# Attention over packs and a two-matrix FFN on one Trainium2 core: from batch 3 on the first softmax is turned by VectorE and small DMAs, side products stand in pairs, and x @ w_in runs two units ahead

## The chip, the core and the metric

The kernel runs on one core of a Trainium2 chip. Its engines are PE (matmul), ACT (activations, copies, casts), DVE (elementwise work, reductions and transposes of 32x32 blocks), POOL (little used here) and SP, whose queue issues nearly all DMAs. The metric is the device time of one execution in microseconds.

## The reference

Eight batches with eight heads of 64, 576 tokens each. 32 packs per head attend to the tokens; the tokens then attend to the 32 results; what comes out goes through an FFN with 2048 hidden columns.

```python
def sm_attn(qq, kk, vv):                       # softmax(qq kk^T / 8) vv, float32
    s = scale * np.matmul(qq, kk.transpose(0, 1, 3, 2))
    ...
p_packed = sm_attn(p, k, v)                    # 32 rows per head
out = sm_attn(q, p_packed, p_packed)           # 576 rows per head
x = out.transpose(0, 2, 1, 3).reshape(4608, 512)
h = x @ w_in                                   # 512 x 2048
return (h * sigmoid(h)) @ w_out                # 2048 x 512
```

## The kernel before

**Units.** The bulk of the work is 128 units, one for a batch and a block of 128 hidden columns, 16 a batch. x itself is never formed. As a token's row of x is its second softmax (32 shares per head) times the packs, `packs_in` multiplies the packs of a batch with w_in once, a quarter (512 columns) at a time, into `pw`. `h_unit(u)` then multiplies `pw` with the shares `a2` (12 matmuls of 288 columns, the line with `a_hi`, `a_lo`, `pw_hi`, `pw_lo`, L408); ACT takes silu out of PSUM three times (`g`, `g_hi`, and `rest` for the 64 tokens that don't fill a block), and DVE makes `g_lo`, the part that `g_hi` lost in rounding. `out_unit(u)` multiplies `g` with w_out (12 matmuls of 512 columns, L422) and sums in PSUM over the 16 units of a batch. Every second batch has four more units for the rest rows (`(b, f, "rest")`).

**Side work.** During the units of batch b the attention of batch b + 1 is made by the generator `side`, piece by piece: scores of packs and keys in two halves (`heads`, L212), maximum on DVE, exponentials on ACT (L251), ten transposes of the exponentials on PE (L274, L279) with copies back to SBUF, the packed product with the values (L289), one more transpose (L308), the second scores in two halves (L212), their softmax (DVE turns blocks of 32, so that a token's 32 shares lie in a row), and four quarters of `packs_in` (L212). Each piece has one two-bank PSUM buffer from a ring of one (`ps_side`); x @ w_in has another (`ps_hid`), and the output sums have the remaining four banks (`ps_acc`).

**Order.** In the first 32 units (batches 0 and 1, `BLOCKS`, while the weights come in and are put together by `Weights`), a scheduler orders all engines by its own estimate of times. Afterwards PE follows the source (`manual_schedule` for PE alone), and the other engines' order is still the scheduler's. `h_unit(u + 1)` stands ahead of `out_unit(u)`: the distance is one unit.

**Start.** Before the first unit, `keep_warm` puts blocks of matmuls on the identity between the pieces of batch 0's attention (`WARM`: 16, 7, 3, 4 and 3 of them, then 10). Each takes a new buffer `ps_hid`. Of a float32 matmul there are two records in the trace. Loads, scalings (L168, L169) and joins (L174 to L178) of the weights are pinned behind named steps (`PINS`).

Of the kernel before, what the change touches and what calls it, by code (L numbers as in the profile page):

```python
# [9 lines left out]
F32 = mybir.dt.float32  # L10
F32R = mybir.dt.float32r
# [3 lines left out]
AF = mybir.ActivationFunctionType  # L15
ALU = mybir.AluOpType
AX = mybir.AxisListType
PSUM = bass.MemoryType.PSUM

P = 128  # L20
B, H, S, D = 8, 8, 576, 64
NP = 32
NI = H // 2
HS = S // 2
NB = HS // 32
# [3 lines left out]
NJ = 4  # L29
JW = DFF // NJ  # L30
FJ = JW // P
# [5 lines left out]
EARLY = 2  # L37
BLOCKS = [(0, 0), (0, 1), (1, 0), (1, 1), (1, 2), (0, 2), (0, 3), (1, 3)]
# [13 lines left out]
A1 = range(0, 6)  # L52
A2 = range(15, 32)
KV2 = 12
SCALE = 1.0 / math.sqrt(D)
EPS = 1e-9

# [4 lines left out]
def packed_attention_ffn(ctx: ExitStack, tc: tile.TileContext, pkT, qT, vA, vB, w_in, w_out, out):  # L62
# [10 lines left out]
    nc = tc.nc  # L73
    ent = ctx.enter_context
    const = ent(tc.tile_pool(name="const", bufs=1))
    kvq = ent(tc.tile_pool(name="kvq", bufs=2))
    pw = ent(tc.tile_pool(name="pw", bufs=2))
    a2p = ent(tc.tile_pool(name="a2p", bufs=4))
    tmp = ent(tc.tile_pool(name="tmp", bufs=2))
    small = ent(tc.tile_pool(name="small", bufs=2))  # L80
    gp = ent(tc.tile_pool(name="gp", bufs=2))
# [14 lines left out]
    made = {}  # L96

    def keep_warm(times):

        with after("pe"):  # L100
            for _ in range(times):
                ps = ps_h.tile([P, 2, 512], F32, name="ps_hid")
                made["pe"] = nc.tensor.matmul(ps[:, 0, :P], ident, ident, start=True, stop=True)  # L103

    def after(name):
        return tc.issue_after(made[name].ins) if name in made else nullcontext()

    def load_pk(b):
        t = kvq.tile([P, 5 * DM], F32, name="kvq_t")
        n = P + NI * HS  # L110
        for c in (slice(0, n), slice(n, n + NI * HS)) if b == 0 else (slice(0, P + NI * S),):
            nc.sync.dma_start(t[:, c], pkT[b, :, c])
        return t[:, :P], t[:, P : P + NI * S].rearrange("p (hf i s) -> p hf i s", hf=2, i=NI)

    def load_q(b):
        t = kvq.tile([P, 5 * DM], F32, name="kvq_t")
        n = NI * HS
        for c in (slice(0, n), slice(n, 2 * n)) if b == 0 else (slice(0, 2 * n),):
            made["q_load", b] = nc.sync.dma_start(t[:, c], qT[b, :, c])
            if b == 0 and c.start == 0:  # L120
                weights.fetch(1)
        return t[:, : NI * S].rearrange("p (hf i s) -> p hf i s", hf=2, i=NI)

    def load_v(b):
        t = kvq.tile([P, 5 * DM], F32, name="kvq_t")
        nc.sync.dma_start(t[:, : 4 * DM], vA[b])
        nc.sync.dma_start(t[: S - 4 * P, 4 * DM :], vB[b])
        return t.rearrange("p (c e) -> p c e", c=5)

    class Weights:  # L130
# [7 lines left out]
        def __init__(self, stage):  # L138
            self.stage, self.raw, self.n, self.fetched = stage, {}, 0, 0

            rings = [["stage", "stage", NJ - 2, NJ - 1], ["stage", "stage", NJ - 1], ["stage", "stage"]]
            self.place, self.after = [], []
            for n in range(len(self.chunks)):
                first = (0, 8, 12)[(n >= 8) + (n >= 12)]
                ring = rings[(n >= 8) + (n >= 12)]
                place = ring[(n - first) % len(ring)]
                before = [m for m in range(n) if self.place[m] == place]
                self.after.append((before[-2:-1] if place == "stage" else before[-1:]) or [-3])
                self.place.append(place)
# [51 lines left out]
    def side_banks(b):  # L201

        if b:
            return ps_s.tile([P, 2, 512], F32, name="ps_side")
        return ps_acc.tile([P, 2, 512], F32, name="ps_acc")

    def heads(bank, lhs, rhs, n):

        for par in range(2):
            r = slice(D * par, D * par + D)  # L210
            for i in range(NI):
                made["pe"] = nc.tensor.matmul(  # L212
                    bank(par)[NP * i : NP * i + NP, :n], lhs(r, i), rhs(r, i), start=True, stop=True
                )

    def scratch(n):
        return tmp.tile([P, 2 * 5 * P], F32, name="tm")[:, : 2 * n]

    def attention(b):
# [134 lines left out]
            made["kv", b + 1] = k_next, load_v(b + 1)  # L354
        yield

    def load_kv(b):
        made["kv", b] = load_pk(b), load_v(b)

    def packs_in(b, j):  # L360
        ps = side_banks(1)
        heads(lambda par: ps[:, par], made["packs", b], lambda r, i: win[r, j, i, :].bitcast(F32), JW)
        pool = pw if b < EARLY or j in (0, NJ - 1) else pw_b
        hi = pool.tile([P, 2, JW], F32R, name="pw_hi")
        lo = pool.tile([P, 2, JW], F32R, name="pw_lo")
        nc.scalar.copy(hi, ps)  # L366
        nc.vector.tensor_tensor(lo, ps, hi.bitcast(F32), ALU.subtract)  # L367
        made["pw", b, j] = hi, lo

    def side(b):  # L370

        yield from attention(b)
        for j in range(NJ):
            packs_in(b, j)
            yield from [None] * 3

# [8 lines left out]
    behind = {}  # L387
# [2 lines left out]

    def h_unit(u):
        b, f, *more = units[u]
        g_hi = gp.tile([P, 512], F32R, name="g_hi")
        g_lo = gp.tile([P, 512], F32R, name="g_lo")
        hidden[u] = g_hi, g_lo
        if more:
            g = rest[:, f : f + FJ].rearrange("p f e h s -> p (f e h s)")
            nc.scalar.copy(g_hi, g)
            nc.vector.tensor_tensor(g_lo, g, g_hi.bitcast(F32), ALU.subtract)
            return  # L400
        p_hi, p_lo = made["pw", b, f // FJ]
        cols = slice(f % FJ * P, f % FJ * P + P)
        ps = ps_h.tile([P, 2, 512], F32, name="ps_hid")
        for hf in range(2):
            a_hi, a_lo = made["a2", b, hf]
            todo = [(p, a, par) for par in range(2) for p, a in ((p_hi, a_hi), (p_hi, a_lo), (p_lo, a_hi))]
            for n, (p, a, par) in enumerate(todo):
                nc.tensor.matmul(ps[:, hf, :HS], p[:, par, cols], a[:, par], start=(n == 0), stop=(n == len(todo) - 1))  # L408
        g = gp.tile([P, 512], F32, name="g", bufs=1)
        main = ps[:, :, :MAIN]  # L410
        silu = nc.scalar.activation(g.rearrange("p (h s) -> p h s", h=2), main, AF.Silu)  # L411
        nc.scalar.activation(g_hi.rearrange("p (h s) -> p h s", h=2), main, AF.Silu)  # L412
        nc.scalar.activation(rest[:, f, b % 2], ps[:, :, MAIN:HS], AF.Silu)  # L413
        lo = nc.vector.tensor_tensor(g_lo, g, g_hi.bitcast(F32), ALU.subtract)  # L414
        behind[u] = silu, lo
# [48 lines left out]
    def load_parts(b):  # L464
        for h in range(2):
            o = osb.tile([P, 2, DM], F32, name="o")
            nc.sync.dma_start(o, parts[b, h])
            outs["o", b, h] = o
# [31 lines left out]
    steps = iter(STEPS)  # L500
    due = next(steps)
    ahead = attention(1)
    ordered = ExitStack()
    for u in range(len(units)):
        b, f, *more = units[u]
        if u < n_early:
            for _ in range(3 if u in A1 else 1 if u in A2 else 0):
                next(ahead, None)
            while u == due:
                silu, lo = behind[u]  # L510
                with tc.issue_after(silu.ins), tc.issue_after(lo.ins):
                    weights.step()
                due = next(steps, None)
            if u % FJ == FJ - 2 and u < n_early - FJ:
                packs_in(*BLOCKS[u // FJ + 1])
            if u == KV2:
                load_kv(2)
                ahead = attention(2)
            if u == n_early - 2:
                packs_in(2, 0)  # L520
            if u % FJ == FJ - 2 and BLOCKS[u // FJ] in ((0, NJ - 1), (1, NJ - 1)):
                load_parts(b)
        else:
            if u == n_early:
                ordered.enter_context(tc.manual_schedule(engines={mybir.EngineType.PE}))
                scope.close()
                pw_b = ent(tc.tile_pool(name="pw_b", bufs=2))
            if u < n_early + FJ - 1:
                packs_in(2, u - n_early + 1)
            if not more and f == 0:  # L530
                for _ in ahead:
                    pass
                ahead = side(b + 1) if b + 1 < B else iter(())
            if not more:
                next(ahead, None)
        if u + 1 < len(units):
            h_unit(u + 1)
        if u >= n_early and not more:
            next(ahead, None)
        out_unit(u)  # L540
    ordered.close()


def _laid_out(q, k, v, p, moe_w_in, moe_w_out):
# [37 lines left out]
```

## Time and profile before

| | us |
|---|---|
| median of 3 runs | 766.7 (765.19 to 766.7) |
| profiled execution | 764.94, its span 763.1 |
| PE busy | 740.8 (97%) |
| weight load (PEld) busy | 580.8 (76%) |
| ACT busy | 345.6 (45%) |
| DVE busy | 328.3 (43%) |
| mean granted clock | 0.981 |

The shares are of the span. A matmul's record includes its way through the array and overlaps the next one's, so the distance between starts says more about PE than the busy share. Where the prediction shows rows of the chain of waits, the columns are the start, the length, and the engine with the tile and line of what was on the chain; rows of the timeline have the start, the length, engine and line, operation, output and inputs, shapes and count.

### The profile page before, as it was taken

Reading aid. Unit: us, or ns where it says so; the run is one execution under the profiler, and the core shown is the slowest. Engines: PE = TensorE matmul, PEld = TensorE weight load, DVE = VectorE, ACT = ScalarE, POOL = GpSimd, SP = SyncE. Lnnn points to the kernel's source line nnn. Section 1 sums busy time; section 2 is a strip of 40 time slices with the busy share of each in tenths; the row PEclk is TensorE's granted clock in tenths of the full one; section 3 lists DMA queues with packets and bytes.
Section 4 is the critical chain, followed back from the end, with each engine's and each line's share of the span. In section 5 each row is a group of like instructions: output and inputs, shape, how many; then the busy total and the mean of one; then the engine's idle time right before and its main releaser. Section 6 shows DMA issues by size and latency. Waiting matters only on the chain.

```text
span 763.1 us, 11971 instructions
## 1 busy us (share of the span) xinstructions
PE 740.8 (97%) x5102; PEld 580.8 (76%) x5102; DVE 328.3 (43%) x482; ACT 345.6 (45%) x606; POOL 17.2 (2%) x14
## 2 busy tenths in 40 slices
PE   8689999999999999999999999999999999999997
PEld 5357767787776887888778787788778887788886
DVE  1697765555754335233713336232723226221112
ACT  2448655754643545362633535353633536242232
POOL 0020000001000000000000000000000000000000
PEclk9958999999999999999999999999999999999999
DMA  6855251334131211031101211031101200010001
GB/s 247 345 179 207 82 165 56 117 111 178 63 110 56 78 66 63 1 118 67 64 0 56 77 67 63 1 118 66 63 1 56 76 2 1 1 56 1 1 1 69
DMA packets 13012, 60.00 MB, mean 79 GB/s; under 512 B 1440, under 2 KB 1440, under 8 KB 8096
## 3 DMA queue, kind: packets, MB, share of 16 engines
q1 hardware_dynamic: 12864, 59.12, 21.5%
q8 instruction: 40, 0.66, 0.4%
q10 hardware_dynamic: 96, 0.13, 0.1%
q14 instruction: 12, 0.10, 0.0%
HBM read 47.71 MB, written 11.53 MB: 78 GB/s over the span
## 4 chain that ended last, share of the span: by engine, by line
PE 86%; ACT 6%; DVE 5%; issue 2%; POOL 0%; ACTq 0%; POOLq 0%
PE ps_acc L422 49%; PE ps_hid L408 26%; PE ps_side L212 6%; PE ps_hid L103 3%; PE ps_side L289 2%; ACT tm L251 1%; ACT L411 1%; ACT L251 1%; DVE mx L241 1%; ACT g L411 1%; ACT g_hi L412 1%; DVE wo_lo L187 1%; DVE g_lo L414 0%; DVE win L177 0%; PE ps_acc L212 0%
## 5 line engine op out<-in xcount | busy, mean ns | idle before, releaser
L422 PE MATMUL ps_acc<-wo_hi,g_hi 128*128 128x512 f32 x576 | 233.6, 406 | 3.2 <-ACT g_hi L412 2.7
L422 PE MATMUL ps_acc<-wo_lo,g_hi 128*128 128x512 f32 x576 | 227.6, 395 | 0.4 <-DVE wo_lo L187 0.4
L422 PE MATMUL ps_acc<-wo_hi,g_lo 128*128 128x512 f32 x576 | 223.5, 396 | 0.0
L411 ACT ACTIVATE g<-ps_hid 128x512 f32<-128x512 f32 x128 | 76.7, 599 | 251.7 <-PE ps_hid L408 248.0
L414 DVE TENSOR_TENSOR g_lo<-g,g_hi 128x512 fp32r<-128x512 f32 x128 | 89.2, 696 | 233.9 <-ACT g_hi L412 233.9
L408 PE MATMUL ps_hid<-a_hi,pw_hi 128*128 128x288 f32 x512 | 156.2, 305 | 2.4 <-ACT rest L413 2.3
L408 PE MATMUL ps_hid<-a_lo,pw_hi 128*128 128x288 f32 x512 | 152.3, 297 | 2.6 <-DVE a_lo L347 2.6
L408 PE MATMUL ps_hid<-a_hi,pw_lo 128*128 128x288 f32 x512 | 151.5, 296 | 0.0
L422 PEld LDWEIGHTS ps_acc<-wo_hi,g_hi 128*128 128x128 f32 x576 | 108.5, 188 | 48.9 <-issue 19.3
L422 PEld LDWEIGHTS ps_acc<-wo_hi,g_lo 128*128 128x128 f32 x576 | 108.4, 188 | 27.3 <-issue 3.0
L422 PEld LDWEIGHTS ps_acc<-wo_lo,g_hi 128*128 128x128 f32 x576 | 108.8, 189 | 20.6 <-DVE wo_lo L187 0.9
L408 PEld LDWEIGHTS ps_hid<-a_hi,pw_hi 128*128 128x128 f32 x512 | 97.1, 190 | 24.6 <-issue 10.1
L408 PEld LDWEIGHTS ps_hid<-a_lo,pw_hi 128*128 128x128 f32 x512 | 97.2, 190 | 7.0 <-DVE a_lo L347 3.0
L408 PEld LDWEIGHTS ps_hid<-a_hi,pw_lo 128*128 128x128 f32 x512 | 97.1, 190 | 0.0
L412 ACT ACTIVATE g_hi<-ps_hid 128x512 fp32r<-128x512 f32 x128 | 75.9, 593 | 0.0
L367 DVE TENSOR_TENSOR pw_lo<-ps_side,pw_hi 128x1024 fp32r<-128x1024 f32 x32 | 39.0, 1220 | 38.6 <-ACT pw_hi L366 38.6
L366 ACT CAST pw_hi<-ps_side 128x1024 fp32r<-128x1024 f32 x32 | 32.4, 1011 | 32.4 <-PE ps_side L212 17.2
L212 PE MATMUL ps_side<-win,ppT 64*32 64x512 f32 x512 | 39.8, 612 | 4.6 <-DVE win L178 4.6
L103 PE MATMUL ps_hid<-ident 128*128 128x128 f32 x86 | 29.4, 437 | 3.4 <-POOL ident masks.py:199 1.4
L103 PEld LDWEIGHTS ps_hid<-ident 128*128 128x128 f32 x86 | 18.4, 266 | 17.6 <-PE ps_hid L103 11.3
L413 ACT ACTIVATE rest<-ps_hid 128x64 f32<-128x64 f32 x128 | 29.5, 230 | 0.0
L411 ACT ACT_TABLE_LOAD x21 | 26.9, 1283 | 5.4 <-PE ps_hid L408 5.2
(93 smaller groups left out, 463.7 us busy)
## 6 DMA issues: line engine op xcount, KB each, us to landing
kvq_t<-in_pkT SPq DMA_DIRECT2D x7, 1216.0 KB, 5.8
w_raw<-in_w_in SPq DMA_DIRECT2D x8, 1024.0 KB, 5.4
kvq_t<-in_vA SPq DMA_DIRECT2D x8, 1024.0 KB, 5.2
out<-o SPq DMA_DIRECT2D x16, 512.0 KB, 2.8
kvq_t<-in_qT SPq DMA_DIRECT2D x7, 1152.0 KB, 5.3
win<-in_w_out SPq DMA_DIRECT2D x5, 1024.0 KB, 4.8
w_raw<-in_w_out SPq DMA_DIRECT2D x3, 1024.0 KB, 4.8
parts<-o SPq DMA_DIRECT2D x4, 512.0 KB, 5.7
```

The lines of the kernel that those rows point to most:

```text
L103: made["pe"] = nc.tensor.matmul(ps[:, 0, :P], ident, ident, start=True, stop=True)
L212: made["pe"] = nc.tensor.matmul(bank(par)[NP * i : NP * i + NP, :n], lhs(r, i), rhs(r, i), start=True, stop=True)
L251: made["exp"] = nc.scalar.activation(e, s, AF.Exp, bias=nm[:, c], scale=SCALE, accum_out=den[:, c])
L289: made["pe"] = nc.tensor.matmul(psp[NP * i : NP * i + NP, par * D : par * D + D], e1T[:n, par, c, NP * i : NP * i + NP], v[:n, c, h * D : ...
L366: nc.scalar.copy(hi, ps)
L367: nc.vector.tensor_tensor(lo, ps, hi.bitcast(F32), ALU.subtract)
L408: nc.tensor.matmul(ps[:, hf, :HS], p[:, par, cols], a[:, par], start=(n == 0), stop=(n == len(todo) - 1))
L411: silu = nc.scalar.activation(g.rearrange("p (h s) -> p h s", h=2), main, AF.Silu)
L412: nc.scalar.activation(g_hi.rearrange("p (h s) -> p h s", h=2), main, AF.Silu)
L413: nc.scalar.activation(rest[:, f, b % 2], ps[:, :, MAIN:HS], AF.Silu)
L414: lo = nc.vector.tensor_tensor(g_lo, g, g_hi.bitcast(F32), ALU.subtract)
L422: nc.tensor.matmul(bank, g[:, rows], w[:, f], start=(first and n == 0), stop=(last and n == 2))
```

## The change

1. `keep_warm` takes one buffer for a whole block of warm-up matmuls.
2. From batch 3 on, the class `Attention` takes the place of the generator; its steps stand at fixed units of the batch before (`STEPS_AT`: unit number to step). The exponentials of the first softmax are turned by DVE in blocks of 32x32 (`turned1`), and sixteen DMAs from SBUF to SBUF, 32 partitions each, put the blocks where PE's transposes had put them. The ten transposes on PE and the two copies behind them are gone.
3. Both halves of the first scores stand together, likewise those of the second scores, and the quarters 0 and 1, and 2 and 3, of `packs_in` (units `PACKS_NEXT` and `PACKS_OWN`). For this `two_banks` gives the two PSUM buffers `ps_hid` and `ps_side` in turn to side pieces and x @ w_in alike. At these units the unit's `h_unit` is left to the next one, which then makes two.
4. x @ w_in stands two units ahead (`hidden_up_to(u + 2)`), with a third buffer for `g_hi`, `g_lo` and for `pw` (`gp_b`, `pw_b`).
5. From the end of the first 32 units, PE, DVE, ACT and SP all follow the source.

```diff
     def keep_warm(times):
+        ps = ps_h.tile([P, 2, 512], F32, name="ps_hid")
         with after("pe"):
             for _ in range(times):
-                ps = ps_h.tile([P, 2, 512], F32, name="ps_hid")
                 made["pe"] = nc.tensor.matmul(ps[:, 0, :P], ident, ident, start=True, stop=True)
...
+STEPS_AT = {1: "scores1", 2: "exps1", 3: "turned1", 7: "packed", 9: "scores2", 10: "exps2", 11: "shares2", 12: "split2"}
+PACKS_NEXT, PACKS_OWN = 13, 4
...
+    turns = [ps_h, ps_s]
+    def two_banks():
+        turns.reverse()
+        return turns[0].tile([P, 2, 512], F32, name="ps_hid" if turns[0] is ps_h else "ps_side")
...
+        def turned1(self):
+            turn = scratch(S)
+            blocks = turn.rearrange("p (t r x) -> p t r x", r=2, x=NP)
+            for par in range(2):
+                nc.vector.transpose(blocks[:, :, par], self.e1[:, par].rearrange("p (t x) -> p t x", x=NP))
+            self.e1T = scratch(5 * P).rearrange("p (c i rx) -> p c i rx", c=5, i=NI)
+            for i in range(NI):
+                for at in range(P // NP):
+                    some = turn[NP * i : NP * i + NP].rearrange("p (t rx) -> p t rx", rx=2 * NP)[:, at :: P // NP]
+                    nc.sync.dma_start(self.e1T[NP * at : NP * at + NP, : some.shape[1], i], some)
...
+    def packs_in(b, *quarters):
+        banks = [side_banks(1) if (b, j) < (EARLY, 1) else two_banks() for j in quarters]
+        for j, ps in zip(quarters, banks):
+            heads(lambda par: ps[:, par], made["packs", b], lambda r, i: win[r, j, i, :].bitcast(F32), JW)
+        for j, ps in zip(quarters, banks):
+            ...   # hi on ACT, lo on DVE, as before
...
+    ent(tc.manual_schedule(engines={E.PE, E.DVE, E.Activation, E.SP}))
...
+        all_banks = step in ("scores1", "scores2") or f == PACKS_OWN or f == PACKS_NEXT and b + 1 < B
+        if not all_banks:
+            hidden_up_to(u + 2)
+        if f == 0 and b + 1 < B:
+            coming = Attention(b + 1)
+        if f == PACKS_OWN:
+            packs_in(b, *((3,) if b == 2 else (2, 3)))
+        if f == PACKS_NEXT and b + 1 < B:
+            packs_in(b + 1, 0, 1)
+        if step:
+            getattr(coming, step)()
         out_unit(u)
+        if step == "packed":
+            coming.packs()
```

**The start on PE**, with buffer numbers: the last warm-up matmuls of the first block, then the first scores, before.

```order
L103 MATMUL ps_hid_137<-ident_88 128x128
L103 MATMUL ps_hid_139<-ident_88 128x128
L103 MATMUL ps_hid_141<-ident_88 128x128
L212 MATMUL ps_acc_143<-kvq_t_103 32x288 x4
L212 MATMUL ps_acc_144<-kvq_t_103 32x288 x4
```

The same place in the changed kernel, from its first matmul to the second block of warm-ups.

```order
L107 MATMUL ps_hid_111<-ident_88 128x128 x16
L223 MATMUL ps_acc_128<-kvq_t_103 32x288 x4
L223 MATMUL ps_acc_129<-kvq_t_103 32x288 x4
L223 MATMUL ps_acc_128<-kvq_t_103 32x288 x4
L223 MATMUL ps_acc_129<-kvq_t_103 32x288 x4
L107 MATMUL ps_hid_146<-ident_88 128x128 x7
```

The matmuls are the same; sixteen buffers have become one.

**Ahead of the first products, on DVE**: `a_lo` is the second half of batch 0's shares, `mx` the maximum of batch 1's first scores, `wo_lo` a part of w_out. Before:

```order
L342 STREAM_TRANSPOSE tm<-tm 128x576
L233 COPY tm<-ps_side 128x2x288
L187 TENSOR_TENSOR wo_lo<-win,wo_hi 128x1024
L241 TENSOR_REDUCE mx<-tm 128x2
L347 TENSOR_TENSOR a_lo<-tm,a_hi 128x576
```

and in the changed kernel:

```order
L181 TENSOR_SCALAR win<-win 128x1024
L244 COPY tm<-ps_side 128x2x288
L358 TENSOR_TENSOR a_lo<-tm,a_hi 128x576
L252 TENSOR_REDUCE mx<-tm 128x2
L191 TENSOR_TENSOR wo_lo<-win,wo_hi 128x1024
```

The scheduler has put `a_lo` ahead of the other two. On ACT, at the same place, before (L251 are batch 1's exponentials, `g` and `g_hi` the first unit's silu):

```order
L251 ACTIVATE tm,den<-tm,nm 128x576 x2
L411 ACT_TABLE_LOAD
L411 ACTIVATE g<-ps_hid 128x512
L412 ACTIVATE g_hi<-ps_hid 128x512
L413 ACTIVATE rest<-ps_hid 128x64
```

and now:

```order
L538 ACT_TABLE_LOAD
L538 ACTIVATE g<-ps_hid 128x512
L539 ACTIVATE g_hi<-ps_hid 128x512
L540 ACTIVATE rest<-ps_hid 128x64
L172 ACTIVATE w_raw<-w_raw 128x1024
L173 ACTIVATE w_raw<-w_raw 128x1024
L172 ACTIVATE w_raw<-w_raw 128x1024
L173 ACTIVATE w_raw<-w_raw 128x1024
L190 CAST wo_hi<-win 128x1024
L262 ACT_TABLE_LOAD
L262 ACTIVATE tm,den<-tm,nm 128x576 x2
L538 ACT_TABLE_LOAD
```

The exponentials have moved from ahead of the first silu to between the first and the second.

**A steady batch.** On PE, one quarter of the packs' product before, between output matmuls (`ps_acc`) and x @ w_in (`ps_hid`):

```order
L422 MATMUL ps_acc<-wo_lo,g_hi 128x512
L422 MATMUL ps_acc<-wo_hi,g_lo 128x512
L212 MATMUL ps_side<-win,ppT 32x512 x8
L408 MATMUL ps_hid<-a_hi,pw_hi 128x288
L408 MATMUL ps_hid<-a_lo,pw_hi 128x288
```

and two quarters in the changed kernel:

```order
L549 MATMUL ps_acc<-wo_hi,g_lo 128x512
L223 MATMUL ps_side<-win,ppT 32x512 x8
L223 MATMUL ps_hid<-win,ppT 32x512 x8
L549 MATMUL ps_acc<-wo_hi,g_hi 128x512
L549 MATMUL ps_acc<-wo_lo,g_hi 128x512
```

The two stand together, in both buffers, between two units' output matmuls. On DVE, from the first scores to the packed product, before:

```order
L241 TENSOR_REDUCE mx<-tm 128x2
L242 TENSOR_SCALAR nm<-mx 128x2
L253 TENSOR_SCALAR rd<-den 128x2
L254 RECIPROCAL rd<-rd 128x2
L414 TENSOR_TENSOR g_lo<-g,g_hi 128x512
L280 COPY tm<-ps_side 64x2x128
L414 TENSOR_TENSOR g_lo<-g,g_hi 128x512 x2
L297 TENSOR_TENSOR pp<-ps_side,rd 128x128
```

and now:

```order
L385 TENSOR_REDUCE mx<-tm 128x2
L386 TENSOR_SCALAR nm<-mx 128x2
L541 TENSOR_TENSOR g_lo<-g,g_hi 128x512 x2
L397 TENSOR_SCALAR rd<-den 128x2
L398 RECIPROCAL rd<-rd 128x2
L541 TENSOR_TENSOR g_lo<-g,g_hi 128x512
L406 STREAM_TRANSPOSE tm<-tm 128x18x32 x2
L500 TENSOR_TENSOR pw_lo<-ps_hid,pw_hi 128x1024
L500 TENSOR_TENSOR pw_lo<-ps_side,pw_hi 128x1024
```

The two turns (L406) are new; the rounding rests of two quarters of `pw` now stand right behind them. On SP the sixteen DMAs (L411) stand between a batch's query load and the next batch's load of packs and keys.

More of the change, by code (lines that the diff above doesn't have):

```diff
@@ L357, in load_kv @@
     def load_kv(b):
         made["kv", b] = load_pk(b), load_v(b)
[L360 to L375, printed above, removed]
+    def packs_in(b, *quarters):
[3 more added lines that the diff above has]
+        for j, ps in zip(quarters, banks):
+            n = NJ * (b - EARLY) + j
+            pool = pw_b if n > 0 and n % 3 == 1 else pw
+            hi = pool.tile([P, 2, JW], F32R, name="pw_hi")
+            lo = pool.tile([P, 2, JW], F32R, name="pw_lo")
+            nc.scalar.copy(hi, ps)
+            nc.vector.tensor_tensor(lo, ps, hi.bitcast(F32), ALU.subtract)
+            made["pw", b, j] = hi, lo
@@ L392, in h_unit @@
         b, f, *more = units[u]
-        g_hi = gp.tile([P, 512], F32R, name="g_hi")
-        g_lo = gp.tile([P, 512], F32R, name="g_lo")
+        pool = gp_b if u > n_early and (u - n_early) % 3 == 1 else gp
+        g_hi = pool.tile([P, 512], F32R, name="g_hi")
+        g_lo = pool.tile([P, 512], F32R, name="g_lo")
         hidden[u] = g_hi, g_lo
@@ L402, in h_unit @@
         cols = slice(f % FJ * P, f % FJ * P + P)
-        ps = ps_h.tile([P, 2, 512], F32, name="ps_hid")
+        ps = ps_h.tile([P, 2, 512], F32, name="ps_hid") if u < n_early else two_banks()
         for hf in range(2):
@@ L502, in packed_attention_ffn @@
     ahead = attention(1)
-    ordered = ExitStack()
-    for u in range(len(units)):
-        b, f, *more = units[u]
[L506 to L523, printed above, removed]
-            if u == n_early:
[L525 to L539, printed above, removed]
@@ new lines, in packed_attention_ffn @@
+    for u in range(n_early):
+        b, f = units[u]
+        for _ in range(3 if u in A1 else 1 if u in A2 else 0):
+            next(ahead, None)
+        while u == due:
+            silu, lo = behind[u]
+            with tc.issue_after(silu.ins), tc.issue_after(lo.ins):
+                weights.step()
+            due = next(steps, None)
+        if u % FJ == FJ - 2 and u < n_early - FJ:
+            packs_in(*BLOCKS[u // FJ + 1])
+        if u == KV2:
+            load_kv(2)
+            ahead = attention(2)
+        if u == n_early - 2:
+            packs_in(2, 0)
+        if u % FJ == FJ - 2 and BLOCKS[u // FJ] in ((0, NJ - 1), (1, NJ - 1)):
+            load_parts(b)
+        h_unit(u + 1)
+        out_unit(u)
@@ new lines, in packed_attention_ffn, with hidden_up_to @@
+    for _ in ahead:
+        pass
+    E = mybir.EngineType
+    ent(tc.manual_schedule(engines={E.PE, E.DVE, E.Activation, E.SP}))
+    scope.close()
+    pw_b = ent(tc.tile_pool(name="pw_b", bufs=1))
+    gp_b = ent(tc.tile_pool(name="gp_b", bufs=1))
+    done = n_early
+    def hidden_up_to(u):
+        nonlocal done
+        while done < min(u, len(units) - 1):
+            done += 1
+            h_unit(done)
+    coming = None
+    for u in range(n_early, len(units)):
+        b, f, *more = units[u]
+        if more:
+            if u == n_early:
+                packs_in(2, 1, 2)
+            else:
+                hidden_up_to(u + 2)
+            out_unit(u)
+            continue
+        step = STEPS_AT.get(f) if b + 1 < B else None
+        all_banks = step in ("scores1", "scores2") or f == PACKS_OWN or f == PACKS_NEXT and b + 1 < B
+        if not all_banks:
+            hidden_up_to(u + 2)
+        if f == 0 and b + 1 < B:
[6 more added lines that the diff above has]
+            getattr(coming, step)()
@@ L540, in packed_attention_ffn @@
         out_unit(u)
-    ordered.close()
+        if step == "packed":
+            coming.packs()
 def _laid_out(q, k, v, p, moe_w_in, moe_w_out):
```

95 lines of the change are left out of this document (added).

## Prediction

> **What bounds the kernel now.** I read the page first, then the windows by stage, then the chain of waits in one steady batch and in the start, then PE's timeline around single pieces.
>
> ```profile
> span 763.1 us, 11971 instructions
> PEclk9958999999999999999999999999999999999999
> PE 86%; ACT 6%; DVE 5%; issue 2%; POOL 0%; ACTq 0%; POOLq 0%
> ...
> 0.00:76.00 76.00, 63.04 (x463) 41.72 (x463) 46.55 (x69) 36.15 (x50) 7.73 (x9) 0.82 0.66 244
> 435.60:517.67 82.07, 81.80 (x604) 65.33 (x604) 31.53 (x49) 37.48 (x70) 0.00 (x0) 1.00 0.16 58
> ```
>
> PE carries 86% of the chain. In a steady batch it has work for 81.80 of 82.07 us, while DVE (31.53) and ACT (37.48) are under half busy: only taking work or gaps out of PE's own stream shortens that part. The first 76 us are different: 13 us without PE work, and a mean clock of 0.82.
>
> **Steady part: the price of a side piece.** The chain of waits in that batch, then PE's timeline around the transposes of the first softmax:
>
> ```profile
> 455.95 2.79 PE ps_acc L422 x12
> 458.74 1.70 PE ps_hid L408 x12
> 460.44 0.65 PE ps_side L212 x16
> 461.09 2.97 PE ps_acc L422 x12
> 464.06 1.02 PE ps_side L212 x16
> 465.08 1.80 PE ps_hid L408 x12
> ...
> 499.65 1.59 PE ps_hid L408 x12
> ...
> 517.45 0.22 PE ps_side L279 x2
> ...
> 514.29 1.03 PE L274 MATMUL ps_side<-ident,tm 128*128 128x128 f32 x8
> 515.59 0.40 PE L408 MATMUL ps_hid<-a_hi,pw_hi 128*128 128x288 f32 x1 [0.27 <-ACT rest L413]
> ```
>
> Undisturbed, a unit is 1.59 (twelve x @ w_in matmuls) and 2.79 (twelve output matmuls), 4.38 us; sixteen are 70.1, so this batch spends 12.0 on side work. A quarter of the packs' product costs 1.02, and the L408 group behind it takes 1.80 instead of 1.59: 1.23. A score piece costs 0.65 + 2.97 - 2.79 = 0.83. The transposes cost more than their matmuls: from 514.29 to 517.45 pass 3.16 us with one L408 group in them, so 1.57 with ACT's 0.27; L279 adds 0.22, and some 0.1 to the group behind it, half of what a longer piece adds: 1.9 a batch.
>
> Two pieces that stand together slow the group behind them once instead of twice (0.2 saved) and let the array run empty once. For the second there are rows at half clock, two score pieces together and one alone, which lasts to the next start:
>
> ```profile
> 14.96 2.10 PE ps_acc L212 x32
> ...
> 43.27 1.21 PE L212 MATMUL ps_side<-kvq_t 64*32 64x288 f32 x16
> 44.41 1.65 PE L103 MATMUL ps_hid<-ident 128*128 128x128 f32 x4
> ```
>
> 2 x 1.14 - 2.10 = 0.18. A merged pair saves 0.2 + 0.17 = 0.37; bounds 0.18 (one effect alone) and 0.5.
>
> **Terms of the steady part**, batches 3 to 7:
> - Transposes off PE: 5 x 1.9 = 9.4 us; bounds 5 x 1.0 (their matmuls alone) and 5 x 2.0.
> - Merged pairs: two of scores and two of quarters a batch, 20 x 0.37 = 7.4; bounds 3.6 and 10. Quarters 1 to 3 of batch 2 stay single in PE's order.
> - x @ w_in two units ahead: the two L408 groups a batch that take 1.70 because ACT has not emptied the bank lose 0.11 each: 1.
> - DVE gains two transposes of 128x576 and loses one copy; ACT loses a copy of 128x1024 and, as the exponentials stand in pairs, two table loads. Both engines are under half busy, so this costs nothing while their order holds (a rival below).
> Together 17.8 us.
>
> **The sixteen small DMAs** of a batch, 32 partitions with runs of 256 bytes, have no like in the trace. Nearest are the stores out of SBUF from the same queue:
>
> ```profile
> L459 SPq DMA_DIRECT2D out<-o x16: 372/394/401, 214.1 to 749.1; - x16
> L439 SPq DMA_DIRECT2D out<-o x14: 332/418/2013, 247.5 to 760.2; - x14
> ...
> DMA to landing us min/median/max: 1.6/2.7/5.0
> ...
> L342 DVE STREAM_TRANSPOSE tm<-tm 128x576 f32<-128x576 f32 x2 | 1.5, 774 | 0.0
> ```
>
> L459 has 256 runs, against 160 or 128 here, so I take its 0.39 an issue: 6.3, and 2.7 to land, 9.0 us; bounds 16 x 0.33 + 1.6 = 6.9 and 16 x 2.01 + 5.0 = 37. What covers it: the exponentials stand in the unit after the scores, behind two silus and a table load, and DVE's two turns (1.55) behind them and the g_lo of the third unit; an estimate from the order puts their end 6.7 us into that unit. The packed product stands behind the seventh unit's L408 group, 4 x 4.38 + 2.1 (two quarters) + 1.59 = 21.2 after the same point. That leaves 14.5 us for 9.0: cost 0. Behind the turns on DVE stand the two pw_lo of the quarters, whose banks PE wants one output group later; behind the DMAs on SP only the next batch's packs and keys, wanted ten units later.
>
> **The start.** The chain of waits of the first 80 us, a window, the first loads and ACT:
>
> ```profile
> 1.36 0.81 PE ps_hid L103 x2
> ...
> 21.14 0.44 PE ps_acc L264 x4
> ...
> 29.02 0.73 PE ps_acc L212 x16
> ...
> 51.22 1.38 DVE wo_lo L187
> 52.60 1.26 DVE mx L241
> 53.87 0.66 DVE a_lo L347
> ...
> 54.70 1.63 ACT tm L251 x4
> ...
> 56.35 1.28 ACT L411
> ...
> 58.78 2.07 PE ps_acc L422 x4
> 60.85 2.34 PE ps_hid L408 x12
> ...
> 65.27 0.93 PE ps_acc L422 x4
> ...
> 30.00:54.50 24.50, 16.77 (x96) 8.43 (x95) 24.33 (x35) 10.57 (x12) 5.13 (x2) 0.60 0.52 181
> ...
> 0.73 0.87 SPq L112 DMA_DIRECT2D kvq_t<-in_pkT  x2
> 2.12 0.59 SPq L126 DMA_DIRECT2D kvq_t<-in_vA  x1
> ...
> kvq_t<-in_vA SPq DMA_DIRECT2D x1, 1024.0 KB, 9.7
> kvq_t<-in_pkT SPq DMA_DIRECT2D x1, 640.0 KB, 3.9
> kvq_t<-in_pkT SPq DMA_DIRECT2D x1, 576.0 KB, 4.8
> ...
> 9.80 1.10 ACT L169 ACTIVATE w_raw<-w_raw 128x1024 f32<-128x1024 f32 x1
> ```
>
> The change's words do not tell of this term. Each of the first sixteen warm-up matmuls takes a new buffer from a ring of one and so waits for the one before: 13.6 us to 14.96, while the keys, issued by 1.6 and 4.8 in flight, had landed by 6.4. The change gives all sixteen one buffer. Back to back a record takes 0.11 (0.44 for four), or 0.22 at half clock, so 32 end between 5 and 8.4.
>
> From there, step by step. The first exponentials stand on ACT behind the first weight scaling, which ends at 10.9 and does not move; the first ends near 11.8, and the transposes run then instead of at 21.14 (seven more warm-ups held them, 4.1 us from 17.06). Copies and values (landed by 12.4) allow the packed product near 14.6, and two shorter warm-up blocks the second scores near 18 instead of 29.02: 11 us earlier. From there to a_lo's end at 54.53 DVE is the bound, busy 24.33 of 24.50 us, and its new order puts wo_lo (1.38) and the maximum (1.26) behind a_lo: a_lo ends near 41. On ACT the first silu no longer stands behind batch 1's exponentials, so products start near 44 instead of 58.78. Then ACT gives part back: between the first and the second silu it now has four scalings (4.4), a cast of about 1, two table loads (2.6) and the exponentials (1.6), so the second unit's products come near 54.3 instead of 65.27. Of that shift of 11 I take off 1 for PE waits behind ACT: **10 us**; bounds 0 (loads set the pace) and 13. Further on the early order is nearly the old one, so the shift stays.
>
> A rule of the Trainium skill speaks against the shorter warm-up: "TensorE: Matmul & The Clock Gate", section "What's actually happening", has PE fall to half clock after an idle window of about 3.4 us, and back after as long a busy one. The trace agrees that the clock falls (PEclk shows 5 in its third slice). By that rule the longer idle stretches of the new start keep the clock down longer: the third rival.
>
> **Sum.** 17.8 + 10 = 27.8 off the profiled execution's 764.94 (its span 763.1 and 1.8 around it): 737.1. The median of the runs, 766.7, lies 1.8 above that execution, so **739 us**.
>
> **Rivals.**
> - *The small DMAs land late* (slower than before). PE then waits at the packed product of five batches. The whole gain is gone when they take 14.5 + 27.8 / 5 = 20 us, which is 1.1 us an issue. The 2.01 in L439's row speaks for it, both medians against it. At 2.01 an issue: 16 x 2.01 + 2.7 - 14.5 = 20.4 a batch, 739 + 102 = 841.
> - *The start does not shorten*, as its loads set the pace: 749. For it: the DMA engines are busy 0.66 of the first 76 us. Against: PE, not a load, is what the chain waits for until 21 us, and a third of the DMA time is free.
> - *The clock stays at half* through the second unit's products and the next L408 group: 2.8 + (2.34 - 1.59) = 3.5 more: 743.
> - *Source order costs on ACT and DVE.* The banks of two quarters come free after two casts on ACT and two pw_lo on DVE, and the L408 groups behind take those banks at once. If a table load's 1.28 shows up there twice a batch, 5 x 2.6 = 13: 752. By my count of the order about 1 us is to spare there, no more.
>
> **Chances.** Forecast 0.57 (its own range 733 to 745), start unchanged 0.15, source order 0.13, clock 0.07, late DMAs 0.08, of which 0.02 near the point of balance. A measurement tells about 0.2% from no change, 1.5 us. So faster 0.92, same 0.02, slower 0.06. The range goes from 732 (start at 13 and pairs near 0.5) to 754 (source order and a little more).
>
> **What would show it.** Right: a steady batch takes 78.5 us instead of 82.07; no L274 rows from batch 3 on; the first score pieces start before 9 us, the second unit's products near 54. Wrong: PE idle ahead of the packed product with a DMA as releaser, or ahead of the x @ w_in group with pw_lo or rest as releaser; warm-ups still 0.85 apart.

## The result, and the profile after

The changed kernel takes 744.72 us (median of four runs, 743.33 to 745.56) against 765.95 for the kernel before (764.95 to 766.7) beside it: ratio 0.9722, 95% interval 0.9699 to 0.9745. The gain is 21.2 us where 27.8 were forecast; 739 was the forecast time, 732 to 754 its range. The profiled execution took 743.93, its span 742.1. From the page of the profile after:

```profile
span 742.1 us, 11983 instructions
PEclk9779999999999999999999999999999999999999
PE 89%; DVE 5%; ACT 4%; DMA 1%; issue 1%; SPq 0%; ACTq 0%
```

PE still carries the chain. I cut both executions at two places, called marks below: the first output matmul, and the first output matmul of the 33rd unit, where the order of the scheduler ends. In rows by stretch the columns are the stretch, its length, the busy time and records of PE, PEld, DVE, ACT and POOL, the granted clock, the share of the DMA engines and GB/s. First the two rows of before, then the two of after:

```profile
58.78:231.14 172.36, 168.56 (x1170) 129.01 (x1171) 110.19 (x147) 103.21 (x162) 11.35 (x6) 0.99 0.34 118
231.14:763.10 531.96, 526.44 (x3623) 424.45 (x3623) 185.12 (x284) 219.82 (x414) 0.00 (x0) 1.00 0.13 46
```

```profile
45.40:227.42 182.02, 171.66 (x1194) 131.68 (x1195) 111.92 (x150) 110.09 (x171) 11.80 (x6) 0.98 0.34 121
227.42:742.10 514.68, 510.43 (x3557) 420.61 (x3557) 188.32 (x289) 200.71 (x397) 0.00 (x0) 1.00 0.16 53
```

So the part behind the second mark lost 17.3 us. The first products came 13.4 us earlier (58.78 to 45.40), but the units between the marks took 9.7 longer, so the start kept 3.7. These two numbers still hold a shift of work across the second mark: between the marks after has 24 matmul records more than before (1194 to 1170), and 16 of them are a quarter of batch 2's packs' product. It stands behind the mark in before, at 234.12, and ahead of it in after, at 223.80 (the mark is at 227.42):

```profile
234.12 1.09 PE L212 MATMUL ps_side<-win,ppT 64*32 64x512 f32 x16
```

```profile
223.80 1.09 PE L223 MATMUL ps_hid<-win,ppT 64*32 64x512 f32 x16
```

It is worth about 1.2 us: e2 and e5 below hold these 16 records more than before and take 173.52 and 173.53 between the marks, before 172.36. With it on the same side in both kernels the steady part lost about 16.1 us (17.8 forecast), and the start kept about 4.9 of the 10 forecast. This is the place where the expected time went.

A steady batch, its row by stretch and pieces of its chain of waits (start, length, what):

```profile
411.41:490.29 78.88, 78.88 (x595) 64.58 (x594) 32.25 (x50) 34.03 (x66) 0.00 (x0) 1.00 0.19 62
```

```profile
414.37 0.65 PE ps_side L223 x16
415.01 0.48 PE ps_hid L223 x16
415.50 2.98 PE ps_acc L549 x12
...
428.84 1.02 PE ps_hid L223 x16
429.86 0.86 PE ps_side L223 x16
```

78.88 us against 82.07, 3.19 less (five such batches make 16.0), and PE has work for all of it. In a pair the second piece takes 0.48 instead of 0.65, or 0.86 instead of 1.02, and the group behind is slowed once. A pair of quarters then costs 1.02 + 0.86 + 0.19 = 2.07 instead of 2 x 1.23, a pair of scores 0.65 + 0.48 + 0.19 = 1.32 instead of 2 x 0.83: 0.39 and 0.34 saved, 0.37 forecast.

The start, rows of PE's timeline (start, length, engine and line, what, count, and the idle time before it with its releaser):

```profile
1.35 6.20 PE L107 MATMUL ps_hid<-ident 128*128 128x128 f32 x32 [1.35 <-POOL ident masks.py:199]
7.49 1.20 PE L223 MATMUL ps_acc<-kvq_t 64*32 64x288 f32 x32
...
45.40 1.22 PE L549 MATMUL ps_acc<-wo_hi,g_hi 128*128 128x512 f32 x2 [1.17 <-ACT g_hi L539]
...
52.95 1.42 PE L285 MATMUL ps_side<-ident,tm 128*128 128x128 f32 x8 [0.50 <-ACT tm L262]
56.11 0.50 PE L549 MATMUL ps_acc<-wo_hi,g_hi 128*128 128x512 f32 x1 [1.74 <-ACT g_hi L539]
...
73.73 0.40 PE L535 MATMUL ps_hid<-a_hi,pw_hi 128*128 128x288 f32 x1 [1.17 <-ACT pw_hi L499]
74.99 0.33 PE L319 MATMUL ps_side<-ident,pp 128*128 128x128 f32 x1 [0.73 <-DVE pw_lo L500]
77.82 0.50 PE L549 MATMUL ps_acc<-wo_hi,g_hi 128*128 128x512 f32 x1 [0.53 <-ACT g_hi L539]
86.06 0.50 PE L549 MATMUL ps_acc<-wo_hi,g_hi 128*128 128x512 f32 x1 [2.94 <-ACT g_hi L539]
```

The warm-ups end at 7.55 instead of 14.96, the first scores start at 7.49. Of the waits from 73.73 on, before has the like of one only (0.53 behind `g_hi`, at 83.16). Ahead of the last one ACT's timeline reads:

```profile
79.98 1.28 ACT L343 ACT_TABLE_LOAD   x1
82.93 0.68 ACT L343 ACTIVATE tm<-tm 128x576 f32<-128x576 f32 x1 [1.67 <-DVE tm L340]
83.63 1.28 ACT L538 ACT_TABLE_LOAD   x1
84.92 0.60 ACT L538 ACTIVATE g<-ps_hid 128x512 f32<-128x512 f32 x1
```

The second softmax of batch 1, with a table load on each side, stands ahead of a silu whose product PE wants at once. The stretch in which the time is given back, before and after:

```profile
58.78:107.72 48.94, 46.73 (x355) 34.64 (x355) 39.91 (x56) 36.82 (x52) 3.79 (x2) 0.96 0.38 131
```

```profile
45.40:103.93 58.53, 49.76 (x367) 37.34 (x368) 41.65 (x59) 42.18 (x59) 4.23 (x2) 0.93 0.39 135
```

It is 9.6 us longer: 8.8 instead of 2.2 without PE work, and 3.0 more of PE work. Of the latter 1.42 are eight transposes that before stood ahead of the first products (L285, the row at 52.95), and about 1.0 are four records of a quarter that in before come just behind this stretch; the granted clock is also lower, 0.93 instead of 0.96.

### The profile page after: what moved, and what is told of

The parts are those of the page before. It is cut to its first block, busy times and chain, and to the rows that moved or that the text cites. A ratio compares the mean times of both kernels' runs of the same rounds, so it can differ in the third digit from the quotient of the medians.

```text
span 742.1 us, 11983 instructions
## 1 busy us (share of the span) xinstructions
PE 710.4 (96%) x5052; PEld 573.0 (77%) x5052; DVE 332.7 (45%) x487; ACT 330.6 (45%) x593; POOL 16.7 (2%) x14
## 4 chain that ended last, share of the span: by engine, by line
PE 89%; DVE 5%; ACT 4%; DMA 1%; issue 1%; SPq 0%; ACTq 0%
PE ps_acc L549 53%; PE ps_hid L535 17%; PE ps_side L535 10%; PE ps_side L223 4%; PE ps_hid L223 2%; PE ps_hid L420 1%; DMA w_raw<-in_w_in 1%; DVE win L179 1%; PE ps_side L300 1%; ACT L538 1%; ACT g L538 0%; DVE pw_lo L500 0%; ACT g_hi L539 0%; ACT w_raw L172 0%; ACT w_raw L173 0%
## 5 line engine op out<-in xcount | busy, mean ns | idle before, releaser
L549 PEld LDWEIGHTS ps_acc<-wo_hi,g_hi 128*128 128x128 f32 x576 | 108.6, 189 | 51.4 <-issue 17.8
L535 PE MATMUL ps_hid<-a_hi,pw_hi 128*128 128x288 f32 x320 | 96.6, 302 | 6.2 <-ACT a_hi L357 4.1
L535 PE MATMUL ps_hid<-a_lo,pw_hi 128*128 128x288 f32 x320 | 95.9, 300 | 2.1 <-DVE a_lo L358 2.1
L535 PE MATMUL ps_hid<-a_hi,pw_lo 128*128 128x288 f32 x320 | 95.6, 299 | 0.0
L535 PEld LDWEIGHTS ps_hid<-a_lo,pw_hi 128*128 128x128 f32 x320 | 61.3, 192 | 4.9 <-DVE a_lo L358 2.3
L535 PE MATMUL ps_side<-a_lo,pw_hi 128*128 128x288 f32 x192 | 56.6, 295 | 0.0
L535 PE MATMUL ps_side<-a_hi,pw_hi 128*128 128x288 f32 x192 | 56.6, 295 | 0.0
L535 PE MATMUL ps_side<-a_hi,pw_lo 128*128 128x288 f32 x192 | 56.5, 294 | 0.0
L535 PEld LDWEIGHTS ps_side<-a_hi,pw_hi 128*128 128x128 f32 x192 | 36.1, 188 | 1.8
L535 PEld LDWEIGHTS ps_side<-a_lo,pw_hi 128*128 128x128 f32 x192 | 36.1, 188 | 1.8
L535 PEld LDWEIGHTS ps_side<-a_hi,pw_lo 128*128 128x128 f32 x192 | 36.1, 188 | 0.0
```

The costliest lines, as they stand in the source:

```text
L549: nc.tensor.matmul(bank, g[:, rows], w[:, f], start=(first and n == 0), stop=(last and n == 2))
```

## Experiments

My theory, T: the one buffer moves the start as forecast, and the scheduler's new early order (batch 1's exponentials between the first silus, a quarter of the packs' product right ahead of its user) gives most of it back. The rival, R: the weights' loads and the work on them set the pace there, so that time won earlier is only waited out elsewhere. Beside that, each term of the steady part was undone alone. Where an experiment is read by its stretches, this is one profiled execution; the medians stand beside it. For the kernel before, the medians beside these runs are 764.97 to 765.19.

**e1_before_one_buffer**: the kernel before with the first part of the change alone.

```diff
     def keep_warm(times):
+        ps = ps_h.tile([P, 2, 512], F32, name="ps_hid")
         with after("pe"):
             for _ in range(times):
-                ps = ps_h.tile([P, 2, 512], F32, name="ps_hid")
```

> The kernel before with one edit: keep_warm takes one buffer for a block. Nothing else changes, but the scheduler orders the first 32 units anew. The forecast's step gives 10 us off (755.9 against 765.9 for the kernel before). Theory T, from the trace after (the early start is won, but the new early order gives most of it back by the 32nd unit, where after stands 3.7 us ahead of before): 3.7 to 5 off, 761 to 762.3. Rival R (the 3.7 us are not from this edit, and the start is set by its loads): within 1.5 of 765.9.

760.26 us, ratio 0.9935 (0.9916 to 0.9955): 4.7 off, as T has it. The first products start at 45.20, and again the units behind them take long:

```profile
45.20:225.98 180.78, 171.77 (x1178) 132.24 (x1179) 112.33 (x150) 108.27 (x169) 11.80 (x6) 0.97 0.34 121
```

180.78 instead of 172.36, in a kernel whose units beyond the 32nd are untouched (532.02 behind the second mark, 531.96 in before). The loss belongs to this edit: of 13.6 us the start keeps 5.2 (231.14 to 225.98).

**e2_after_ring**: the changed kernel with this part undone (the diff above the other way round).

> The changed kernel with the ring for the warm-ups put back: each of them takes a new buffer. Theory T: 3.7 to 5 slower than after, 748.4 to 749.7, first products near 58.8 and the steady part, from the first unit after the scheduled 32 to the end, 514.7 as in after. The forecast's step: 10 slower, 754.7. Rival R: no change, 744.7.

749.83 us, 0.9793 (0.9776 to 0.9811), 5.1 above after's 744.72. The first products start at 60.71, the scheduled units take 173.52, and the rest 514.77, as in after (514.68). By medians both ways of asking give the edit 5 us, not 10. The profiled executions put e2 further off, its second mark 6.8 us behind after's (234.23 to 227.42); but the profiled one is e2's slowest (750.82), and its first products come 1.9 later than before's.

**e5_pins**: the early start with nearly the early order of before.

```diff
 PINS = (
-    ("", "nm"),
+    (("exp0"), ("tT", 0)),
...
+            if b == 0:
+                made["exp0"] = made["exp"]
```

> The changed kernel with two pins more: the first weight scaling stands behind batch 0's exponentials, and the first join of a weight behind the first copy of the turned exponentials. The scheduler then keeps the one buffer's early start and goes back to nearly the early order of before: a quarter of the packs' product stands one output group ahead of its user, and batch 1's exponentials ahead of the first silu. Theory T (the new early order, not the loads, gives the early start back: 8.8 us without PE work between 45.4 and 103.9 against 2.2 in the like stretch of before): up to 5 faster than after, 740 to 742. Rival R (the weights' loads and the work on them set the pace up to about 104 us, so that PE only waits elsewhere): within 1 of 744.7.

739.17 us (738.76 to 739.81), 0.9655 (0.9639 to 0.9671): faster than after, whose interval begins at 0.9699. The matmuls are after's (eight records fewer lie between the two marks, transposes that now stand ahead of the first), and the stretch behind the second mark is as long as there:

```profile
48.65:222.18 173.53, 169.73 (x1186) 129.12 (x1187) 110.22 (x147) 104.47 (x164) 11.35 (x6) 0.99 0.34 120
222.18:737.00 514.82, 510.54 (x3557) 420.53 (x3557) 188.30 (x289) 200.70 (x397) 0.00 (x0) 1.00 0.16 53
```

The first products start 3.25 us later than in after, since batch 1's exponentials again stand ahead of the first silu, and yet the 33rd unit starts 5.2 earlier. The 2.94 behind `g_hi` and the waits ahead of x @ w_in and the next transpose behind `pw_hi` and `pw_lo` (1.17 and 0.73) are gone; the same weights are loaded. The clock is no rival here: its mean from 38 to 62 us is 0.72 in both. R is refuted for these 5 us, and T shown, as far as the order as a whole goes: with nearly the order of before, the start keeps 9.0 us (231.14 to 222.18), and 10.1 with the quarter's 1.2, which is the forecast's 10.

**e6_quarter_earlier**: of T's two places, the quarter alone.

```diff
-        if u % FJ == FJ - 2 and u < n_early - FJ:
+        if u % FJ == FJ - 3 and u < n_early - FJ:
```

> The changed kernel with the quarters of the packs' product one unit earlier in the scheduled units, nothing else. Theory T by its rows: the waits behind pw_hi and pw_lo (1.17 and 0.73) go, the waits behind g_hi (1.74, 0.53, 2.94) shift but stay in part: 1.5 to 3 faster, 742 to 743. If the exponentials with their table loads ahead of a silu are the whole cause: within 1 of 744.7. Rival R: within 1 of 744.7.

741.59 us, 0.9697 (0.9671 to 0.9723), 3.1 below after, with an interval that overlaps after's. Between the marks:

```profile
46.88:225.10 178.22, 171.75 (x1195) 131.63 (x1195) 112.03 (x150) 109.77 (x171) 11.81 (x6) 0.97 0.35 123
```

3.8 us shorter than in after, though the first products start 1.5 later (46.88 to 45.40; the last section shows such a shift), so the second mark comes 2.3 earlier. The order of the second softmax moved with the quarter (the wait of 2.94 is gone too, one of 1.54 behind a DMA has come in its place), so this does not divide the loss between the two places.

**e12_pins_and_quarter_earlier**: both edits together.

> The version with the two pins (739.2), and the quarters of the packs' product one unit earlier in the scheduled units. If both edits cure the same waits, as theory T has it (a quarter directly ahead of its user): no more than the pins alone, 738 to 740. If they cure different ones, their gains add: 739.2 - 3.1 = 736.

739.33 us, 0.9658 (0.9639 to 0.9677); between the marks 173.54, in e5 173.53. The gains do not add, as T has it. The waits that are left are not the same ones, though: 1.5 us behind a DMA here, which e5 does not have.

**e11_pins_and_later_scaling**: the two pins, and

```diff
-STEPS = [0, 0, 1, 2, 4, 7, 10, 12, 14, 17, 19, 21, 23]
+STEPS = [0, 1, 1, 2, 4, 7, 10, 12, 14, 17, 19, 21, 23]
```

> The version with the two pins (739.2), and one chunk of the weights' scaling later, behind the second silu. Theory T, that ACT between the first two silus is what is left: the products start at 48.65 as there and the second and third units come up to 2 earlier, 737 to 739. Rival R (the late chunk's user, the fourth part of the weights, is then the one that waits): 740 to 743.

741.98 us, 0.9699 (0.9679 to 0.972): 2.8 above the pins alone, where R has it by its number. The products start at 48.57, the scheduled units take 175.67, with a wait of 0.57 behind `g_hi` at 89.76 and one of 1.53 behind a DMA at 96.76. So ACT between the first two silus is not what is left. R's mechanism is not shown: PE has no wait for a weight there. What the trace has beside the two waits is a granted clock of 0.50 from 96.45 to 103.28, where e5 has 1.00; what made it fall stays open.

**e3_turns_on_pe**: the transposes back on PE, two units later (`STEPS_AT` with 5 instead of 3 for `turned1`).

```diff
-                nc.vector.transpose(blocks[:, :, par], self.e1[:, par].rearrange(...))
...
-                    nc.sync.dma_start(self.e1T[...], some)
+                for c in range(4):
+                    nc.tensor.transpose(pst[:, par, c * P : c * P + P], self.e1[:, par, c * P : c * P + P], ident)
...
+        if step == "turned1":
+            coming.turned1_rest()        # the two of the last 64 tokens, behind out_unit(u)
```

> The changed kernel with the first softmax of batches 3 to 7 turned by PE again: eight transposes ahead of the fifth unit's output matmuls and two behind them, each lot with its copy (ACT, DVE); VectorE's turns and the sixteen DMAs are gone, all else stays. The forecast's term: 5 x 1.9 = 9.4 slower, 754.1. By the transposes' matmuls alone (its lower bound): 5 slower, 749.7. If the small DMAs or the turns cost time that I have not seen: less than 5 slower, or faster.

751.31 us, 0.9821 (0.9799 to 0.9844), 6.6 above after by medians. Behind the second mark:

```profile
227.00:747.30 520.30, 516.01 (x3607) 425.63 (x3607) 183.59 (x284) 205.23 (x402) 0.00 (x0) 1.00 0.13 47
```

50 records and 5.6 us more than in after: 1.12 a batch, near the forecast's lower bound of 1.0, not 1.9.

**e4_pairs_apart** and **e7_pairs_apart_early**: the pairs taken apart, the second piece behind the unit's output matmuls (e4), or the first piece one unit earlier (e7); the scores and a batch's own quarters likewise.

```diff
-        if f == PACKS_NEXT and b + 1 < B:
-            packs_in(b + 1, 0, 1)
+        if f == PACKS_NEXT and b + 1 < B:          # e4; e7: f == PACKS_NEXT - 1
+            packs_in(b + 1, 0)
...
         out_unit(u)
+        if f == PACKS_NEXT and b + 1 < B:          # e4; e7: f == PACKS_NEXT, ahead of out_unit(u)
+            packs_in(b + 1, 1)
```

> The changed kernel with the twenty pairs taken apart: the second half of the scores and the second quarter of a pair stand behind the unit's output matmuls. The forecast's term: 20 x 0.37 = 7.4 slower, 752.1. By the trace after (a pair of quarters saves 0.39, a pair of scores 0.34): 7.3. One effect alone (the group behind, or the emptying of the array): 3.6 to 4, 748.5. If the two buffers that go to a pair hold up the L420 groups, so that standing apart relieves them: under 3.

759.48 us, 0.9925 (0.9908 to 0.9942): 14.8 above after, twice the forecast. The chain behind such a quarter:

```profile
438.46 1.10 PE ps_side L223 x16
...
439.58 1.02 ACT pw_hi L511
...
440.63 1.24 DVE pw_lo L512
...
441.91 1.86 PE ps_side L547 x12
```

With the output matmuls ahead of the second quarter instead of behind it, nothing covers its evacuation, 1.02 on ACT and 1.24 on DVE, and x @ w_in needs that buffer next. This edit undid more than the pairs, so e7:

> The changed kernel with the twenty pairs taken apart the other way: the first half of the scores and the first quarter of a pair stand one unit earlier, ahead of that unit's output matmuls, so that no evacuation is closer to its user than in after. If the 14.8 us of the former experiment are the pairs' price (7.3) and PE's waits for the buffers that the second pieces hold: about 7.3 slower than after, 752, and no wait of x @ w_in for pw_lo. If standing apart costs 14.8 by itself: 759.5.

752.01 us, 0.9828 (0.9807 to 0.985): 7.3 above after, as expected, with no wait for `pw_lo` behind the mark. Behind the second mark it takes 521.59, 6.9 more than after, with the same 3557 records.

**e9_one_unit_ahead**: `hidden_up_to(u + 1)` instead of `u + 2`.

> The changed kernel with x @ w_in one unit ahead instead of two, from the end of the scheduled units on; the pairs stay. The forecast's term: two L408 groups a batch lose 0.11 each again, about 1 slower, 745.7. Theory T2 (the distance is what makes room for the pairs: with one unit, PE stands at a pair's group with no x @ w_in in hand, and the silu behind it is exposed): more, at about 1.2 to 2 us a pair and 20 pairs, 770 to 785. If the distance does nothing: 744.7.

746.69 us, 0.976 (0.9736 to 0.9783); behind the mark 517.16, 2.5 more than after. T2 falls: the pairs do not need the distance. By distances between starts, 66 of 93 groups of twelve output matmuls take 2.9 us instead of 2.8, in after 47 of 95. The list of waits behind the mark has a row that after's has not, of PE's weight loads:

```profile
PEld ps_acc L549 <- DVE g_lo L541: 5.8, 21, 0.3
```

Of these 21 waits 19 stand in such longer groups, at the third matmul, the first that reads `g_lo`; and 66 is 19 more than 47. So with one unit's distance `g_lo` comes too late now and then, at 0.1 us each time. Before has no such wait, so these 2.5 us are a price of one unit in the changed kernel, not a time that before lost. What before lost there, and neither after nor e9 does, stands in two rows of before's list:

```profile
PEld ps_hid L408 <- ACT rest L413: 5.4, 15, 0.5
PE ps_hid L408 <- ACT rest L413: 1.4, 5, 0.3
```

**e8_turns_one_unit_later**: `STEPS_AT` with 4 instead of 3 for `turned1`.

> The changed kernel with VectorE's turns and so the sixteen DMAs of batches 3 to 7 one unit later, behind the two pw_lo of the quarters: about 4.2 to 4.7 us later, the packed product at its place. By the trace of after its DMAs land 2.3 us ahead of the packed product: PE then waits about 2 us in each of five batches, 9.5 to 12 slower, 754 to 757. By the forecast's cover (5.5 us to spare): no change, 744.7.

752.52 us, 0.9828 (0.9807 to 0.9848). In after, the sixteen DMAs of the batch shown (SP's timeline) and all 80, with the time that an issue takes:

```profile
430.69 10.75 SPq L411 DMA_DIRECT2D tm<-tm  x16
```

```profile
L411 SPq DMA_DIRECT2D tm<-tm x80: 593/602/1437, 263.1 to 610.3; - x80
...
DMA to landing us min/median/max: 1.9/1.9/3.7
```

In e8 those of the same batch are issued from 440.96 on, and PE's timeline and the list of waits read:

```profile
451.75 0.31 PE L420 MATMUL ps_hid<-kvq_t,tm 128*32 128x64 f32 x6
452.86 1.68 PE L420 MATMUL ps_hid<-kvq_t,tm 128*32 128x64 f32 x74 [0.79 <-DMA tm<-tm]
```

```profile
PE ps_hid L420 <- DMA tm<-tm: 5.2, 5, 1.4
```

Relative to the packed product the issues moved by 4.1 us: from 14.9 ahead of it (430.69 to 445.57) to 10.8 (440.96 to 451.75). PE waits 5.2 in five batches, 1.04 each, so in after about 3.1 were to spare. Behind the mark e8 takes 521.22, 6.5 more; the expected 9.5 came from a margin of 2.3 read off the issue and landing times, 0.8 too small. The rest of the 10.2 us between the two profiled executions (752.3 to 742.1) lies ahead of the mark; 2.5 of it, at the start, is taken up in the last section.

**e10_source_order_pe_alone**:

```diff
-    ent(tc.manual_schedule(engines={E.PE, E.DVE, E.Activation, E.SP}))
+    ent(tc.manual_schedule(engines={E.PE}))
```

> The changed kernel with source order for PE alone in the unscheduled units; DVE, ACT and SP are ordered by the scheduler there, as in the kernel before. The forecast costs the source order on these engines at nothing: 744.7, within 1. The rival of the forecast (source order costs on ACT and DVE): faster than after, by up to 13. If the scheduler, which does not see the DMAs' true times, puts the turns or the DMAs later: slower, by PE's wait at five packed products.

743.85 us, 0.9724 (0.9699 to 0.9749); behind the mark 514.70 against 514.68. The source order on DVE, ACT and SP costs nothing here and brings nothing.

The fastest version that ran is e5_pins, 26 us ahead of the kernel before.

## Why the prediction was right, and where it was not

- **What bounds it, and the steady part**: right. PE's stream alone set it, and what went out of it came out of the time: about 16.1 of 17.8, a batch 78.88 where 78.5 was forecast.
- **Its terms**: pairs 7.4, measured 6.9. Transposes 9.4, measured 5.6 alone: ACT's 0.27 that I counted with them does not return in e3, where no x @ w_in group waits for ACT. Of the 16.1 these two leave 3.6. The third term named the right groups, those of x @ w_in that wait until ACT has emptied their bank, but it was too small, and the distance is not what relieves them. Summed from each start to the next, x @ w_in takes 158.8 us behind the mark in before, 153.7 in after and still 153.8 in e9; e7 and e3 bring back 1.8 and 0.4 of the 5.1. What e9 keeps and before did not have are two buffers in turn for x @ w_in; that they are the cause was not tested.
- **Its price of a pair**: the 0.18 for the array's emptying came from two rows "at half clock". For the one at 14.96 the profile prints a granted clock of 1.00; only its length speaks for half (2.10 us, where the same 32 records in after take 1.20). The steady pair bears the price out: the second of two score pieces takes 0.48 instead of 0.65.
- **The start, 10 us**: the step that failed, and with it the size of the sum. "a_lo ends near 41" and "products start near 44" came out as 42.61 and 45.40 (`a_lo` itself took 2.00 instead of 0.66). What failed is "Of that shift of 11 I take off 1 for PE waits behind ACT" and "Further on the early order is nearly the old one, so the shift stays". I had followed the new order to the second unit (56.11, forecast 54.3) and compared the rest only by eye. It differs there: PE idles 6.6 us more in the 59 us behind its first products than before did in the like stretch. e1, e2 and e5 size the term: about 5 us with the new order, 10 with nearly the old.
- **Small DMAs**: right that they are hidden, wrong in size. The median issue took 0.60 instead of the 0.39 of a store with more runs; issues start about 0.65 apart and one took 1.07, so the sixteen shown took 10.75 instead of 6.3; 3.1 us were to spare instead of 5.5. The lower landing time (1.9 for 2.7) made up a part.
- **The range**: its lower end, 732, lies 1.3 below what its own terms give (738.9 - 3 - 2.6 = 733.3).
- **Rivals**: start unchanged and source order are out by e1 and e10, and late DMAs by the 3.1 us to spare. The clock came in part. PE's clock in 1 us pieces behind the second unit's wait, from the rows by stretch of after:

```profile
55.00:56.00 1.00, 0.00 (x0) 0.00 (x0) 0.00 (x0) 1.00 (x3) 0.00 (x0) 1.00 1.08 369
56.00:57.00 1.00, 0.89 (x4) 0.76 (x5) 0.91 (x2) 1.00 (x3) 0.00 (x0) 1.00 0.87 352
57.00:58.00 1.00, 1.00 (x7) 0.95 (x6) 0.97 (x2) 1.00 (x2) 0.00 (x0) 0.77 0.93 385
58.00:59.00 1.00, 1.00 (x6) 1.00 (x6) 1.00 (x2) 1.00 (x2) 0.00 (x0) 0.50 0.24 98
59.00:60.00 1.00, 1.00 (x5) 1.00 (x5) 0.97 (x2) 0.24 (x2) 0.00 (x0) 0.50 0.10 33
60.00:61.00 1.00, 1.00 (x4) 0.72 (x4) 0.51 (x1) 1.00 (x3) 0.00 (x0) 0.52 0.00 0
```

While PE idles the clock stands at 1.00, and it falls to 0.50 only when PE has been at work again since 56.11 for about one and a half (0.77 is the mean of the piece in which it falls). By these rows it stays there for about 3.4 us, up to 61. There x @ w_in's matmuls start 0.24 apart instead of 0.13, so I estimate the cost at some 1.7 us, of the 3.5 that the rival put on it. That the wait of 1.74 brought the fall is not shown. The Trainium skill ("TensorE: Matmul & The Clock Gate", "What's actually happening") has a free-running window of about 3.4 us judge past activity; that the fall comes late agrees with it, but no unbroken idle time of that length precedes it here: the gaps are 0.50 and 1.74, with 1.42 of transposes between them.

## What to carry to other kernels

When an edit at the start changes what a scheduler thinks of times, its whole order may change, so each group's distance from its user must be compared row by row up to the end of the scheduled part, not only where the edit stands. An earlier first product is no gain by itself: e5 started its products 3.25 us later than after and was 5 us faster. When undoing one part to price it, look at what else it moves: the same pairs cost 14.8 us apart in one place and 7.3 in another, and one unit's distance brought in a wait that the kernel before never had. Before a stretch is compared with its like, its records must be counted: here a quarter had moved across the mark, and with it 1.2 us from one term to another.

## What I had not expected of the hardware

A DMA from SBUF to SBUF with 160 or 128 runs of 256 bytes held its queue 0.60 us an issue (median of 80), although a store with 256 runs took 0.39.

And of the eight kernels with the one buffer and the same order on PE up to the first products (after, e1, e3, e4, e7 to e10), seven started these between 44.98 and 45.44 us, but e8 at 47.94, though its edit lies far behind. The granted clock shows where. In both after and e8 the first packed product starts near 14.7, but from 14 to 21 us after has a clock of 1.00 and e8 one of 0.51 (the last but two of the columns). PE's row of the packed product, then the row by stretch, after and then e8:

```profile
14.77 1.73 PE L300 MATMUL ps_acc<-kvq_t,tm 128*32 128x64 f32 x80 [1.27 <-DVE tm L279]
14.00:21.00 7.00, 5.97 (x133) 4.31 (x134) 4.09 (x9) 2.50 (x4) 0.00 (x0) 1.00 1.02 419
```

```profile
14.70 2.83 PE L300 MATMUL ps_acc<-kvq_t,tm 128*32 128x64 f32 x80 [1.26 <-DVE tm L279]
14.00:21.00 7.00, 6.30 (x95) 5.34 (x95) 2.42 (x6) 2.43 (x4) 0.00 (x0) 0.51 1.03 422
```

The second scores then start at 21.05 instead of 18.51, and the first products are late by the same 2.54 us. e6 has a mean clock of 0.76 in this stretch, and its second scores and its first products are 1.48 late. PE's waits ahead of the packed product are no longer in e8 than in after (1.08 and 1.26 against 1.57 and 1.27), so why the clock falls in one execution and not in another stays open. One profiled start can thus be 2.5 us off; e8's is the slowest of its four executions (754.1, the median 752.52).
